# Products with v in groups of five and four key tiles (first batch: two) instead of three (first batch: one)

## The chip, the cores and the metric

The kernel runs on one core of one Trainium2 chip. The metric is the device time of one execution in microseconds (us); lower is better. Three executions of the kernel before gave 1371.67, 1372.15 and 1375.9 us, so the median is 1372.15 us. Engines are named as the profile names them: PE is TensorE (its matmuls), PEld its weight loads, DVE is VectorE, ACT is ScalarE, POOL is GpSimd, SP is SyncE.

## The reference, cut to what matters

All arrays are 32-bit floats. q, k and v have the shape (4, 8, 1152, 64): 4 batches, 8 heads, 1152 positions, 64 features.

```python
q_pool = q.reshape(B, H, S // 2, 2, D).mean(axis=3)           # 576 queries
scores = (1 / sqrt(D)) * q_pool @ k.transpose(0, 1, 3, 2)
attn = exp(scores - max(scores)); attn = attn / (sum(attn) + 1e-09)
x = (attn @ v), heads side by side                            # (2304, 512)
h = x @ moe_w_in;   x = (h - tanh(h)) @ moe_w_out             # 512 -> 2048 -> 512
h = x @ moe2_w_in;  r = max(h, 0)
out = (s * r * r + b) @ moe2_w_out
```

## The kernel before, in words

The 32 heads are taken as 16 pairs; pair n holds heads (n, 0) and (n, 1), and four pairs (NPAIR) make a batch. For each head a loop runs over nine key tiles t of 128 positions (NKT = 9). `scores` (line 380) makes for each half g of the 576 queries the scores transposed, keys on the partitions: two matmuls (lines 386 and 387) into one PSUM tile of 128x288, and ACT takes its exponential into one half of the tile `pf` (line 388). There are three such PSUM tiles and PFB = 10 `pf` tiles.

The scores and both dense layers run in a reduced 32-bit format (one pass over the 288 columns for each matmul). The products of `pf` with v run in full 32-bit format: for one key tile and one half, the 288 columns go through the array in two matmul records.

The products come in two forms:

- In the first batch (n < 4) v has a 65th column of ones, and `single` (line 451) multiplies one key tile: its half 0 into the PSUM tile `pv`, its half 1 into the PSUM tile `su` (line 458), 65 columns of weights each, so that the sum of the exponentials comes out as a 65th row. Between the two halves there is a tick.
- In the later batches `batch` (line 479) multiplies BATCH = 3 key tiles in one go (line 490), 64 columns of weights each: half 0 goes into PSUM partitions 0 to 63, half 1 into 64 to 127, and the two halves run side by side. The sums of the exponentials are made by POOL, which adds the nine `pf` tiles of a head (line 449), and by one product with ones for each head (line 504, `total`), which is put behind the last batch of the head. Only the last head of all (15, 1) has its sums made by PE (line 428).

`batch` is called when more than BATCH tiles are pending, so it runs behind the scores of the tile after its own; `single` when more than LAG = 3 are pending. `batch` puts its matmuls on PE right behind the last matmul of the scores (`issue_after`, with raised priority).

Everything else is woven in by `tick`, four times for each key tile: it runs what was put off (`later`), a step of `prep` for the pair after the next (transposes of q and k, lines 289 and 308; and the maxima of the scores, whose matmuls at line 347 are reduced by DVE at line 348 through three PSUM tiles of the pool psP), and, in the later batches, 111 ns worth of matmuls of the first dense layers (lines 557 and 570), which use psP as well. DVE also turns weights into the reduced format (lines 209 to 221), POOL takes part in this at line 224.

Behind the attention come the two dense stages (line 700 to the end), which the change does not touch.

Of the kernel before, what the change touches and what calls it, by code (L numbers as in the profile page):

```python
# [9 lines left out]
F32 = mybir.dt.float32  # L10
# [8 lines left out]
P = 128  # L19
# [5 lines left out]
LAG = 3  # L25
# [18 lines left out]
SUM = 2  # L44
GROUPS = ((0, 1, 2, 3, 4, 5, 6, 7, 8),)
GROUPS_LAST = ((0, 1, 2, 3, 4), (5, 6, 7, 8))
BATCH = 3
STORE, PUT = 8, 6

MOE_NS = 445  # L50
EVAC_NS = 250
AHEAD = 400
PFB = 10
SOON = 40
HOLD_NS = 8000

# [6 lines left out]
def attention_moe_moe_kernel(  # L63
# [14 lines left out]
    B, H, S, D = q.shape  # L78
# [3 lines left out]
    SQ = S // 2  # L82
    HB = SQ // 2
    NKT = S // P
# [16 lines left out]
    mm = nc.tensor.matmul  # L101
# [21 lines left out]
    for i in range(4):  # L123
        g = i % 2
# [26 lines left out]
    def later(k, fn):  # L151
        queue.append((clock[0] + k, fn))
# [77 lines left out]
    ap = actx.enter_context(tc.tile_pool(name="att", bufs=1, side="right"))  # L230
# [16 lines left out]
    vos = [ap.tile([P, NKT, D + 1], F32, name=f"vo{i}") for i in range(2)]  # L247
# [132 lines left out]
    def scores(n, j, t):  # L380
        T1, U1 = ops[n]
        pf = ap.tile([P, SQ], F32, tag="pf", name=f"pf{n}_{j}_{t}", bufs=PFB)
        for g in range(2):
# [21 lines left out]
    def groups(n, j):  # L405

        return GROUPS_LAST if (n, j) == (len(pairs) - 1, 0) else GROUPS

    def plain(n, j):

        return (n, j) == (len(pairs) - 1, 1)

    fresh = []
    sums = {}

    def sum_plain(n, j, t0):


        if t0 == 0:
            return  # L420
        if (n, j) not in sums:
            sums[n, j] = psV.tile([P, HB], F32, tag="su", name=f"su{n}_{j}")
        su = sums[n, j]
        while fresh and fresh[0][:2] == (n, j) and fresh[0][2] < t0 + BATCH:
            _, _, u, pf = fresh.pop(0)
            for g in range(2):
                o = 32 * (2 * (u % 2) + g)
                mm(su[o:o + 32], ones[:, 0:32], pf[:, g * HB:(g + 1) * HB],
                   start=(u < 2), stop=(u >= NKT - 2))
        if t0 == NKT - BATCH:  # L430
            later(1, lambda: spread_plain(n, j))

    def spread_plain(n, j):
        sx = fp.tile([P, HB], F32, tag="sx", name=f"sx{n}_{j}")
        act(sx, sums.pop((n, j)), AF.Copy)
        pt = psP.tile([P, KB], F32, tag="pp", name=f"pts{n}_{j}")
        mm(pt[:, :HB], spread, sx, start=True, stop=True)
        end(n, j, pt[:, :HB])

    last = [None]  # L440
    pvt, accs, due = {}, {}, []
    placed = []

    def add(n, j, t, r, pf):

        old = accs[n, j, r]
        if t == groups(n, j)[r][1]:
            accs[n, j, r] = ap.tile([P, SQ], F32, tag="acc", name=f"acc{n}_{j}_{r}", bufs=4)
        added[0] = pool.tensor_add(accs[n, j, r], old, pf)  # L449

    def single():

        n, j, t, pf = pend.popleft()
        if t == 0:
            pvt[n, j] = [psV.tile([P, HB], F32, tag=x, name=f"{x}{n}_{j}") for x in ("pv", "su")]
        po = pvt[n, j]
        for g in range(2):
            mm(po[g][0:D + 1], vos[j][:, t], pf[:, g * HB:(g + 1) * HB],  # L458
               start=(t == 0), stop=(t == NKT - 1))
            yield  # L460
        if t == NKT - 1:
            later(0, lambda: finish_single(n, j))

    def finish_single(n, j):
        xv = xvs[n, j] = fp.tile([P, HB], F32, tag="xv", name=f"xv{n}_{j}", bufs=3)
        po = pvt.pop((n, j))
        for g in range(2):
            act(srow[D:D + 1, g], po[g][D:D + 1], AF.Copy)
            act(xv[g * D:(g + 1) * D], po[g][0:D], AF.Copy)

        def total():
            pt = psP.tile([P, KB], F32, tag="pp", name=f"pts{n}_{j}")
            for g in range(2):
                mm(pt[:, :HB], rows[g], srow[:, g], start=(g == 0), stop=(g == 1))
            end(n, j, pt[:, :HB])

        later(2, total)

    def batch():


        todo = [pend.popleft() for _ in range(BATCH)]
        n, j, t, _ = todo[0]
        if t == 0:
            pvt[n, j] = psV.tile([P, HB], F32, tag="pv", name=f"pv{n}_{j}")
        po = pvt[n, j]
        with tc.high_priority(offset=AHEAD), tc.issue_after(last[0].ins):
            for i, (_, _, u, pf) in enumerate(reversed(todo)):
                for g in (1, 0):
                    mm(po[g * D:(g + 1) * D], vos[j][:, u, 0:D], pf[:, g * HB:(g + 1) * HB],  # L490
                       start=(t == 0 and i == 0), stop=(u == NKT - BATCH))
            total()
            if plain(n, j):
                sum_plain(n, j, t)
        if t == NKT - BATCH:
            later(0, lambda: finish_head(n, j))

    def total():
        for n, j in due:
            su = psV.tile([P, HB], F32, tag="su", name=f"su{n}_{j}")  # L500
            nr = len(groups(n, j))
            for r in range(nr):
                for g in (1, 0):
                    mm(su[g * D:(g + 1) * D], ones, accs[n, j, r][:, g * HB:(g + 1) * HB],
                       start=(r == 0), stop=(r == nr - 1))
            later(0, lambda: end(n, j, su))
        due.clear()
# [3 lines left out]
    def finish_head(n, j):  # L511

        xv = xvs[n, j] = fp.tile([P, HB], F32, tag="xv", name=f"xv{n}_{j}", bufs=3)
        act(xv, pvt.pop((n, j)), AF.Copy)
# [81 lines left out]
    pend = deque()  # L596

    def add_prep(n):
        preps.append([prep(n), clock[0]])
# [4 lines left out]
    def fill(ns):  # L604
        credit[0] += ns
        while moe and credit[0] > 0:
            try:
                ns = next(moe[0])
                credit[0] -= ns
                done[0] += ns if ns == 123 else 0  # L610
            except StopIteration:
                moe.popleft()
        credit[0] = min(credit[0], 0)

    def tick():

        clock[0] += 1
        due = [x for x in queue if x[0] <= clock[0]]
        queue[:] = [x for x in queue if x[0] > clock[0]]
        for _, fn in due:  # L620
            fn()
        for p in list(preps):
            if p[1] <= clock[0]:
                try:
                    p[1] = clock[0] + next(p[0])
                except StopIteration:
                    preps.remove(p)
        if done[0] < total_ns - HOLD_NS:
            fill(MOE_NS / 4)
# [13 lines left out]
    for n in range(len(pairs)):  # L643
        b, hp = pairs[n]
        if n == 0:
            add_prep(1)
        for j in range(2):
            for t in range(NKT):
                if j == 1 and t == NKT - LEAD // 4 and n + 2 < len(pairs):
                    add_prep(n + 2)  # L650
                if t == LAG + 1:
                    if j == 1 and n + 1 < len(pairs):
                        preps.append([prep_head(n + 1, 0), clock[0]])
                    if j == 0 and n > 0:
                        preps.append([prep_head(n, 1), clock[0]])
                if hp == 1 and j == 0 and t == 0 and b > 0:
                    while moe:
                        fill(1000)
                    moe.extend(sweep1(b - 1, g) for g in range(2))
                while (n, j) not in ready:  # L660
                    tick()
                for _ in scores(n, j, t):
                    tick()
                if pend[0][0] < NPAIR:
                    if len(pend) > LAG:
                        for _ in single():
                            tick()
                    else:
                        tick()
                        tick()  # L670
                else:
                    tick()
                    if len(pend) > BATCH:
                        batch()
                    tick()
                if (n, j, t) in early1:
                    with tc.issue_after(newest[0].ins) if n == 0 else ExitStack():
                        w1gen.step()
                if n == len(pairs) - 1 and (n, 1) in ready:
                    if FW not in slots:  # L680
                        pctx.close()
                        wpc = ctx.enter_context(tc.tile_pool(name="wc", bufs=1, reuse_waits="tile"))
                        new_slots(wpc, range(FW, FA))
                    w1gen.step()
# [91 lines left out]
    pend = deque()  # L776
# [50 lines left out]
    for i in range(NBLK):  # L827
# [3 lines left out]
        for f in range(NFC):  # L831
            assert w2gen.left <= 2 * (NFC - 1 - f) or not w2gen.left
            ps = hidden(weight(1, f), cur, NB, f"2_{i}_{f}")
            r = mp_.tile([P, NB], F32, tag="th", name=f"r{i}_{f}")
# [46 lines left out]
```

## Time and profile before

| | |
|---|---|
| median of three runs | 1372.15 us |
| the profiled execution | 1372.28 us, its span 1370.5 us |
| instructions in the span | 22374 |
| PE busy | 1336.5 us, 98% of the span |
| DVE, ACT, POOL busy | 63%, 42%, 30% |
| mean granted TensorE clock | 0.996 |
| products with v, first batch (line 458) | 288 matmul records, from 33.1 to 184.3 us |
| products with v, later batches (line 490) | 864 matmul records, from 185.2 to 639.0 us |

Times in the trace are counted from the start of the span. The attention ends at about 641 us. A matmul's shown duration holds its way through the array, which overlaps the next matmul: what a matmul costs in a full stream is the distance from its start to the next start. A timeline row with "x12" merges twelve neighbours: its start is that of the first, and the next row's start tells when the following matmul began.

### The profile page before, as it was taken

The page shows a single profiled execution, that of the slowest core. Times are in us where ns is not written, and L with a number is a line of the kernel's source. Part 1 is how long each engine was busy: PE and PEld are TensorE (multiplying, and loading weights), DVE is VectorE, ACT ScalarE, POOL GpSimd, SP SyncE. Part 2 cuts the span into 40 slices and gives each one's busy share as a digit, 9 for nine tenths or more (in the row PEclk, how much of TensorE's full clock was granted, in tenths as well). Part 3 has the DMA queues.
Part 4 walks back from the last instruction along what each step waited for, and adds up shares of the span by engine and source line. Part 5 has one row for each costly group of instructions (what it writes and reads, how often), then busy time and mean ns, then how long its engine had stood idle before and what let it go on. Part 6 is the DMA issues. An engine that isn't in the chain of part 4 may idle for free.

```text
span 1370.5 us, 22374 instructions
## 1 busy us (share of the span) xinstructions
PE 1336.5 (98%) x8262; PEld 1153.4 (84%) x8262; DVE 870.1 (63%) x1643; ACT 572.7 (42%) x1408; POOL 411.7 (30%) x333
## 2 busy tenths in 40 slices
PE   7999998999999999998999999999999999999998
PEld 4777766777777777776999999999999999989997
DVE  6887779776566665768898668886873232323332
ACT  2455554555555555553333333443332222323222
POOL 0221166667677666773222111110120000000000
PEclk9999999999999999999999999999999999999999
DMA  8677766575656666454785226665421101010000
GB/s 187 150 167 167 168 143 141 133 180 135 165 112 157 139 152 152 100 130 120 249 254 191 97 66 194 203 200 166 158 79 37 47 24 46 24 46 24 1 24 23
DMA packets 190413, 169.58 MB, mean 124 GB/s; under 512 B 88928, under 2 KB 166880, under 8 KB 190304
## 3 DMA queue, kind: packets, MB, share of 16 engines
q1 hardware_dynamic: 187968, 167.56, 46.4%
q8 instruction: 65, 1.06, 0.3%
q10 hardware_dynamic: 2336, 0.59, 0.2%
q14 instruction: 44, 0.36, 0.1%
HBM read 101.98 MB, written 30.67 MB: 97 GB/s over the span
## 4 chain that ended last, share of the span: by engine, by line
PE 86%; DVE 7%; DMA 3%; issue 1%; ACT 1%; POOL 0%; SPq 0%; ACTq 0%; DVEq 0%; POOLq 0%
PE h L744 26%; PE o L817 15%; PE y L755 11%; PE pv L490 7%; PE ptm L347 5%; PE s L386 5%; PE s L387 5%; PE y L570 3%; PE h L557 3%; PE pv L458 2%; PE su L458 2%; DVE ri L523 1%; PE ptk L308 1%; DVE mp L348 1%; DMA raw<-in_moe_w_out_dram 1%
## 5 line engine op out<-in xcount | busy, mean ns | idle before, releaser
L744 PE MATMUL h<-xx,w 128*128 128x288 f32 (+1 forms) x2256 | 373.3, 314 | 0.9 <-DMA xx<-x1d 0.9
L744 PEld LDWEIGHTS h<-xx,w 128*128 128x128 f32 x2256 | 350.6, 188 | 8.9 <-DMA xx<-x1d 1.1
L388 ACT ACTIVATE pf<-s 128x288 f32<-128x288 f32 x576 | 219.1, 410 | 139.0 <-PE s L387 131.5
L348 DVE TENSOR_REDUCE mp<-ptm 128x1 f32<-128x384 f32 x384 | 204.0, 548 | 89.7 <-PE ptm L347 81.4
L449 POOL TENSOR_TENSOR acc<-acc,pf 128x576 f32<-128x576 f32 x159 | 229.6, 1444 | 61.5 <-ACT pf L388 53.8
L224 POOL TENSOR_TENSOR w<-t,w 128x512 fp32r<-128x512 f32 (+1 forms) x80 | 89.1, 1114 | 428.5 <-ACT w L223 278.4
L386 PE MATMUL s<-U,T 128*128 128x288 f32 x576 | 185.9, 330 | 1.5 <-ACT pf L388 0.9
L755 PE MATMUL y<-ghb,w 128*128 128x288 f32 x784 | 171.8, 296 | 0.0
L387 PE MATMUL s<-U,T 65*128 65x288 f32 x576 | 171.5, 307 | 0.1
L817 PE MATMUL o<-w,g2h 128*128 128x512 f32 x540 | 169.3, 395 | 0.0
L347 PE MATMUL ptm<-T,U 128*128 128x384 f32 x360 | 139.4, 393 | 6.3 <-DVE mp L348 3.1
L836 DVE SCALAR_TENSOR_TENSOR r<-r,sb 128x384 f32<-128x384 f32 x96 | 59.2, 618 | 134.2 <-ACT r L835 134.1
L755 PEld LDWEIGHTS y<-ghb,w 128*128 128x128 f32 x784 | 130.4, 188 | 0.2 <-DVE yr L763 0.2
L841 DVE SCALAR_TENSOR_TENSOR g2l<-r,sb,g2h 128x384 fp32r<-128x384 f32 x96 | 61.3, 638 | 105.7 <-ACT g2h L840 105.7
L386 PEld LDWEIGHTS s<-U,T 128*128 128x128 f32 x576 | 111.2, 194 | 18.0 <-ACT pf L388 6.2
L490 PE MATMUL pv<-pf,vo 128*64 128x288 f32 x864 | 121.0, 415 | 0.0
L387 PEld LDWEIGHTS s<-U,T 65*128 65x128 f32 x576 | 110.8, 194 | 7.2 <-issue 4.4
L817 PEld LDWEIGHTS o<-w,g2h 128*128 128x128 f32 x540 | 100.6, 188 | 16.9
L755 PE MATMUL y<-glb,w 128*128 128x288 f32 x392 | 114.6, 292 | 0.0
L835 ACT ACTIVATE r<-h 128x384 f32<-128x384 f32 x96 | 47.1, 491 | 154.1 <-PE h L744 153.7
L817 PE MATMUL o<-w,g2l 128*128 128x512 f32 x270 | 106.9, 396 | 0.0
L840 ACT ACTIVATE g2h<-r,sb 128x384 fp32r<-128x384 f32 x96 | 59.4, 619 | 111.5 <-PE o L817 107.9
(102 smaller groups left out, 1886.1 us busy)
## 6 DMA issues: line engine op xcount, KB each, us to landing
xx<-x1d SPq DMA_DIRECT2D x80, 288.0 KB
T<-T SPq DMA_DIRECT2D x50, 288.0 KB
raw<-in_moe_w_in_dram SPq DMA_DIRECT2D x23, 512.0 KB
raw<-in_moe_w_out_dram SPq DMA_DIRECT2D x23, 512.0 KB
qr<-in_q_dram SPq DMA_DIRECT2D x32, 288.0 KB
vo<-in_v_dram SPq DMA_DIRECT2D x32, 288.0 KB
x1d<-xo SPq DMA_DIRECT2D x64, 144.0 KB
x2d<-xo SPq DMA_DIRECT2D x32, 288.0 KB
```

Of the source, the lines that this page charges most:

```text
L224: added[0] = pool.tensor_sub(w[:, 2 * i + 1, cols], x, f32(w[:, 2 * i, cols]))
L347: mm(pt, U1[j][:, q0:q0 + P], T1[j][:, kk], start=True, stop=True)
L348: newest[0] = dve.reduce_max(mp[:, s, i:i + 1], pt, axis=AX.X)
L386: last[0] = mm(ps, T1[j][:, t * P:(t + 1) * P], U1[j][:, sl], start=True, stop=False)
L387: last[0] = mm(ps, T2[j][:, t * P:(t + 1) * P], U2[j][:, sl], start=False, stop=True)
L388: act(pf[:, sl], ps, AF.Exp, scale=SCALE)
L449: added[0] = pool.tensor_add(accs[n, j, r], old, pf)
L490: mm(po[g * D:(g + 1) * D], vos[j][:, u, 0:D], pf[:, g * HB:(g + 1) * HB], start=(t == 0 and i == 0), stop=(u == NKT - BATCH))
L744: mm(ps[:, :n], w[:, a, c * P:(c + 1) * P], xx[:, c, x, 0:n], start=(i == 0 and c == 0), stop=(i == 2 and c == NDC - 1))
L755: mm(ys[i][c], w[:, a, c * P:(c + 1) * P], x, start=(f == fa and r == 0), stop=(f == fb - 1 and r == 2))
L817: mm(ys[i][r], x[:, r * P:(r + 1) * P], w[:, a], start=(f == 0 and n == 0), stop=(f == NFC - 1 and n == 2))
L841: dve.scalar_tensor_tensor(out=gl, in0=r, scalar=sb2[:, 1:2], in1=f32(gh), op0=ALU.add, op1=ALU.subtract)
```

## The change

The products with v are taken in other groups. In the later batches a head's nine tiles are taken as five and four (SPLIT), except the last head (15, 1), which keeps three times three (SPLIT_LAST). In the first batch `single` takes two tiles at once (PAIRED; the ninth tile is alone), later one before the other, without a tick between the halves, and right behind the last scores; it is called when more than four tiles are pending instead of three. One more `pf` tile (PFB = 11) is paid for with one fewer accumulator of POOL (`acc`, three instead of four). The accumulation flags follow the groups.

```diff
-BATCH = 3
+SPLIT = (5, 4)
+SPLIT_LAST = (3, 3, 3)
+PAIRED = 2
...
-PFB = 10
+PFB = 11
...
-            accs[n, j, r] = ap.tile([P, SQ], F32, tag="acc", name=f"acc{n}_{j}_{r}", bufs=4)
+            accs[n, j, r] = ap.tile([P, SQ], F32, tag="acc", name=f"acc{n}_{j}_{r}", bufs=3)
...
     def single():
-        n, j, t, pf = pend.popleft()
+        n, j, t, _ = pend[0]
+        todo = [pend.popleft() for _ in range(min(PAIRED, NKT - t))]
         if t == 0:
             pvt[n, j] = [psV.tile([P, HB], F32, tag=x, name=f"{x}{n}_{j}") for x in ("pv", "su")]
         po = pvt[n, j]
-        for g in range(2):
-            mm(po[g][0:D + 1], vos[j][:, t], pf[:, g * HB:(g + 1) * HB],
-               start=(t == 0), stop=(t == NKT - 1))
-            yield
-        if t == NKT - 1:
+        with tc.issue_after(last[0].ins):
+            for _, _, u, pf in reversed(todo):
+                for g in range(2):
+                    mm(po[g][0:D + 1], vos[j][:, u], pf[:, g * HB:(g + 1) * HB],
+                       start=(t == 0 and u == todo[-1][2]), stop=(u == t and todo[-1][2] == NKT - 1))
+        if todo[-1][2] == NKT - 1:
             later(0, lambda: finish_single(n, j))
...
+    def size(n, j, t):
+        split = SPLIT_LAST if plain(n, j) else SPLIT
+        return split[[sum(split[:i]) for i in range(len(split))].index(t)]
+
     def batch():
-        todo = [pend.popleft() for _ in range(BATCH)]
-        n, j, t, _ = todo[0]
+        n, j, t, _ = pend[0]
+        todo = [pend.popleft() for _ in range(size(n, j, t))]
+        end_ = todo[-1][2] == NKT - 1
...
-                       start=(t == 0 and i == 0), stop=(u == NKT - BATCH))
+                       start=(t == 0 and i == 0), stop=(end_ and i == len(todo) - 1))
             total()
             if plain(n, j):
-                sum_plain(n, j, t)
-        if t == NKT - BATCH:
+                sum_plain(n, j, t, todo[-1][2] + 1)
+        if end_:
             later(0, lambda: finish_head(n, j))
...
                 if pend[0][0] < NPAIR:
-                    if len(pend) > LAG:
-                        for _ in single():
-                            tick()
-                    else:
-                        tick()
-                        tick()
+                    tick()
+                    if len(pend) > LAG + PAIRED - 1:
+                        single()
+                    tick()
                 else:
                     tick()
-                    if len(pend) > BATCH:
+                    if len(pend) > size(*pend[0][:3]):
                         batch()
                     tick()
```

## Rows read from the trace of the kernel before

**Rows 1.** Windows: length, busy us (x instructions) per engine, granted clock, DMA share, GB/s.

```profile
33.00:185.00 152.00, 150.09 (x792) 114.38 (x791) 122.67 (x281) 83.85 (x225) 31.05 (x37) 1.00 0.74 166
185.00:262.00 77.00, 68.35 (x431) 51.36 (x431) 62.30 (x108) 38.73 (x107) 54.00 (x42) 0.96 0.56 127
262.00:600.00 338.00, 334.71 (x2275) 263.30 (x2272) 224.55 (x405) 185.03 (x511) 237.07 (x178) 1.00 0.62 143
```

**Rows 2.** Line 490 by itself: its instructions, and its weight loads in two of those windows.

```profile
L490 PE MATMUL pv<-pf,vo x864: 406/406/744, 185.2 to 639.0; 128*64 128x288 f32 x173
...
185.00:262.00 77.00, 19.95 (x142) 9.39 (x144) 0.96 0.56 127
262.00:600.00 338.00, 89.28 (x640) 40.90 (x636) 1.00 0.62 143
```

**Rows 3.** PE timeline (start, us, line, tiles, count), a batch of three tiles alone.

```profile
610.99 0.29 PE L387 MATMUL s<-U,T 65*128 65x288 f32 x1
611.21 1.68 PE L490 MATMUL pv<-pf,vo 128*64 128x288 f32 x12
612.82 0.67 PE L557 MATMUL h<-xx,w 128*128 128x288 f32 x3
613.32 0.29 PE L386 MATMUL s<-U,T 128*128 128x288 f32 x1
```

**Rows 4.** PE timeline, a batch with the product with ones behind it.

```profile
600.50 0.30 PE L387 MATMUL s<-U,T 65*128 65x288 f32 x1
600.72 1.68 PE L490 MATMUL pv<-pf,vo 128*64 128x288 f32 x12
602.23 0.66 PE L504 MATMUL su<-acc,ones 128*64 128x288 f32 x4
602.82 0.44 PE L347 MATMUL ptm<-T,U 128*128 128x384 f32 x1
603.09 0.29 PE L570 MATMUL y<-gla,w 128*128 128x288 f32 x1
```

**Rows 5.** PE timeline of the first batch, one tile's products between scores.

```profile
151.07 0.65 PE L458 MATMUL pv<-pf,vo 128*65 128x288 f32 x2
151.56 0.65 PE L458 MATMUL su<-pf,vo 128*65 128x288 f32 x2
...
152.31 0.30 PE L386 MATMUL s<-U,T 128*128 128x288 f32 x1
152.44 0.30 PE L387 MATMUL s<-U,T 65*128 65x288 f32 x1
152.58 0.65 PE L458 MATMUL pv<-pf,vo 128*65 128x288 f32 x2
```

**Rows 6.** The same with two matmuls of line 347 in the round.

```profile
155.49 0.34 PE L347 MATMUL ptm<-T,U 128*128 128x384 f32 x1
155.67 0.29 PE L386 MATMUL s<-U,T 128*128 128x288 f32 x1
...
155.93 0.65 PE L458 MATMUL pv<-pf,vo 128*65 128x288 f32 x2
...
157.78 0.65 PE L458 MATMUL pv<-pf,vo 128*65 128x288 f32 x2
```

**Rows 7.** The two longest waits of PE in 185 to 262 us: total us, times, longest us.

```profile
PE ptm L347 <- DVE tha L584: 2.9, 1, 2.9
PE ptk L308 <- DVE mp L348: 2.4, 1, 2.4
```

**Rows 8.** Waits of PE in 262 to 600 us.

```profile
PE y L570 <- DVE gla L588: 1.0, 3, 0.4
PE ptm L347 <- DVE mp L348: 0.8, 3, 0.3
PE y L570 <- DVE mp L348: 0.4, 2, 0.2
```

**Rows 9.** Waits of PE in 600 to 645 us.

```profile
PE su L504 <- POOL acc L449: 2.9, 1, 2.9
```

More of the change, by code (lines that the diff above doesn't have):

```diff
@@ L414, in attention_moe_moe_kernel, with sum_plain @@
     sums = {}
-    def sum_plain(n, j, t0):
+    def sum_plain(n, j, t0, t1):
         if t0 == 0:
@@ L423, in sum_plain @@
         su = sums[n, j]
-        while fresh and fresh[0][:2] == (n, j) and fresh[0][2] < t0 + BATCH:
+        while fresh and fresh[0][:2] == (n, j) and fresh[0][2] < t1:
             _, _, u, pf = fresh.pop(0)
@@ L429, in sum_plain @@
                    start=(u < 2), stop=(u >= NKT - 2))
-        if t0 == NKT - BATCH:
+        if t1 == NKT:
             later(1, lambda: spread_plain(n, j))
```

## The prediction

> **What bounds the kernel now.** I read the windows first, then the timeline of PE around the products, then the waits. The windows [rows 1] show where PE has no time to spare: in the first batch it is busy for 150.09 of 152 us, in the long middle of the attention for 334.71 of 338 us, while DVE, ACT and POOL each have at least a fifth of the time free. Between 185 and 262 us it is different: PE lacks 8.65 us, and DVE is busy for 62.30 of 77 us. So in the middle a microsecond taken from PE's own stream shortens the run, and in the short stretch it may only lengthen a wait.
>
> Then the price of a matmul as the distance from start to start. A reduced-format matmul of 288 columns costs (152.58 - 152.31) / 2 = 0.135 us, and one full-format record (151.56 - 151.07) / 2 = 0.245 us [rows 5]. A matmul of line 347 costs 155.67 - 155.49 = 0.18 us [rows 6].
>
> **What a group of three costs beyond its matmuls.** From 610.99 to 613.32 us are 2.33 us [rows 3]. In them start four reduced-format matmuls (one of line 387, three of line 557: 0.54 us) and a batch of 12 records. Its halves run side by side, so these are 6 x 0.243 = 1.46 us. 2.33 - 0.54 - 1.46 = 0.33 us are left. They lie at both ends: the batch starts 0.22 us after line 387 instead of 0.135, and the rest comes after it. The batch with the product with ones [rows 4] gives the same: 603.09 - 600.50 = 2.59 us, less 0.135, less 8 x 0.243 = 1.94, less 0.18 for line 347, is 0.33 us. So a batch pays 0.33 us once, whether it has 6 or 8 steps. No engine is named in these rows as late, so this is paid by PE itself on the way into the side-by-side form and out of it.
>
> **Later batches: 23 groups fewer.** Line 490 has 864 records at 12 a batch [rows 2]: 72 batches, three for each of 24 heads. 23 heads go to two, the last keeps three: 49 batches. 23 x 0.33 = 7.6 us less on PE; the number of matmuls stays. All of it lies on the path where PE is the bound. By window: 144 / 12 = 12 batches, four heads, lie in 185 to 262 us; 636 / 12 = 53 in 262 to 600 us [rows 2].
>
> What can eat of this: in 185 to 262 us PE waits 2.9 us once for the gate's subtraction and 2.4 us once for a reduction of the maxima [rows 7], both on DVE. If DVE's chain sets those moments, the four groups saved there (1.3 us) lengthen the waits. The same holds for the one group saved in head (15, 0): PE waits 2.9 us for POOL's last sum [rows 9]. So between 0 and 1.7 us of the 7.6 is lost; without a row that tells which, I take the middle, 0.9 us.
>
> What a longer batch adds: five tiles keep PE away from scores, maxima and dense work for 5 x 2 x 0.243 + 0.33 = 2.8 us instead of 1.8. ACT and DVE run dry for that time, and afterwards PE may wait for them. Today this costs almost nothing: in 262 to 600 us all waits of PE for DVE are 1.0 + 0.8 + 0.4 = 2.2 us [rows 8], 0.04 us for each of the 53 batches. Batches get longer by half and fewer by a third, so I cost this at zero. The bounds are a gain of those 2.2 us and a loss of the same size. The cover is the free third of DVE (224.55 of 338 us) and the 45% of ACT [rows 1]. The call comes, as before, one tile after the group's last scores, so it waits for no younger exponential; and the last group of a head is still called behind the first scores of the next head, so POOL's sums are due at the same tile.
>
> The buffers are costed at nothing. Up to six tiles are pending instead of four, and PFB grows by one, which leaves five `pf` tiles for ACT to run ahead instead of six; ACT runs about one tile ahead. An accumulator lives from a head's second tile to the first tile of the next head, so at most two are alive. If either were short, ACT or POOL would stop for one batch, 2.8 us at most, and PE after them.
>
> **First batch: no switch to save, some evenness to lose.** Here 72 groups become 8 x (4 + 1) = 40, but rows 5 show no price of a group. One round from 151.07 to 152.58 us lasts 1.51 us and holds four reduced-format matmuls (0.54 us) and four records (0.98 us): 1.52 us. With line 347 between the halves [rows 6] there are even two groups in a round: 157.78 - 155.93 = 1.85 us against 0.54 + 0.98 + 0.36 = 1.88 us. With 65 columns the halves do not run side by side, and entering and leaving is free. So nothing is removed on PE.
>
> The Trainium skill agrees on this point: its page TensorEngine Tiling (Key Properties) says that a change of the tiling mode, not of the tile alone, drains TensorE, and under When to Use Tiling it gives 64 columns or fewer as the case for column tiling. By that rule 65 columns change no mode and the 32 groups saved here are worth nothing; by the opposite reading, in which any change of form costs what a batch costs, they would be worth 10.6 us. The rounds above side with the first.
>
> What is added is a wait in line: eight records, 8 x 0.245 = 1.96 us, in one piece instead of two pieces of 0.49 us with a step of line 347 between them. Queued behind them on PE are the next maxima, for which DVE waits, and the next scores, for which ACT waits. DVE is the one to watch: 122.67 of 152 us busy here [rows 1], 81%. The bounds: PE can gain no more than the 1.9 us that it lacks in this window; and at the other end, if DVE had nothing to spare, the additional 4 x 0.245 = 0.98 us of every pair would be lost, 32 x 0.98 = 31 us. The nearest row is the middle of the attention, where pieces of 1.5 to 2 us already interrupt the same loop at 0.04 us each: 32 x 0.04 = 1.3 us. I take that, since it is the same loop with the same three PSUM tiles, and DVE is only somewhat fuller.
>
> **Sum.** -7.6 + 0.9 + 0 + 1.3 = -5.4 us. The profiled execution took 1372.28 us (0.13 us above the median of the three runs), so 1366.9 us. Both dense stages behind the attention keep their length and only start earlier.
>
> **The rivals.**
>
> *The gain is absorbed.* PE gets ahead, and what empties its PSUM tiles does not. For it: the 5.3 us and 2.9 us of waits for DVE and POOL that exist already [rows 7, 9], and that a burst empties DVE's queue. Against it: 2.2 us of such waits in the 338 us that hold 53 of the 72 batches [rows 8]. Here the rest would be 0 to 4 us of gain, in the middle 1370.3 us. The Trainium skill speaks for this rival: TensorEngine Tiling (PSUM Bottleneck) warns that a faster TensorE leaves the emptying of PSUM as it was, and that the copies can become the bound; the windows show that they are not in the middle stretch. To this rival also belongs that the longer groups do not stay whole on PE.
>
> *The first batch gets slower by more than the later ones gain.* One mechanism: in the piece of 1.96 us DVE runs out of maxima, its conversions are queued behind the reductions that it waits for, and the lost time comes back as waits of PE for psP. The later batches bring 7.6 - 0.9 = 6.7 us, so it decides from 6.7 / 32 = 0.21 us per pair; at 0.45 us, half of what a pair can lose, it is 32 x 0.45 = 14.4 us, and the time 1372.28 - 6.7 + 14.4 = 1380.0 us. For it: DVE's 81%. Against it: 29 us of DVE's window are free.
>
> *Every group costs, in the first batch too.* Then 32 x 0.33 = 10.6 us more go: 1372.28 - 6.7 - 10.6 = 1355.0 us. Against it stand the two rounds that add up without it [rows 5, 6].
>
> **How the numbers follow.** Forecast 58%, absorbed 25%, slower 11%, larger gain 6%. About 0.3% is what a measurement of this kernel can tell from no change: 4.1 us, so faster is below 1368.0 us and slower above 1376.3 us. The forecast's own range is 1363 (the full 7.6 us and the 1.9 us of the first batch) to 1369 (1.7 us absorbed and 2.5 us lost in the bursts). Of its 58 some 8 lie above 1368.0; faster is then 50 + 6 + 5 from the upper part of the absorbed cases = 61%. Slower is 9 of the 11; the other 30% are no change. For 8 in 10 the range must take in nearly all of the absorbed case: 1361 to 1373 us. Its low end also lets the wait of rows 9 go.
>
> **What would show it.** Right: line 490 keeps 864 records in 49 batches; a batch of five takes 0.33 us beyond 10 x 0.243 us; PE's busy time falls by about what the time falls; the stretch from 262 to 600 us is shorter by some 5.5 to 6 us, and the stretch from 33 to 185 us longer by 1 to 2 us, with new waits of line 347 for line 348. Wrong: if the first batch gets shorter by more than 2 us, groups there did cost something; if waits of PE for DVE or ACT in the middle grow beyond 4 us, the bursts matter; if a batch of five costs much more than 0.33 us beyond its matmuls, the price is not one for each group.

## The result, and the profile after

The changed kernel took 1383.3 us in the median of five runs (1382.43 to 1389.7) against 1372.15 us: a ratio of 1.0087 [1.0059, 1.0115]. It is slower by 11 us where 5.4 us of gain were forecast, and it lies above the range of 1361 to 1373 us. The profiled execution is the longest of the five, 1389.7 us, with a span of 1387.9 us at a granted clock of 0.989; before had 0.996. A second profile of the same kernel (label x1, below) has a span of 1381.5 us at 0.993.

The windows of [rows 1], now of the changed kernel. The columns are window and length, busy time and instructions of PE, PEld, DVE, ACT and POOL, granted clock, DMA share, GB/s:

```profile
33.00:185.00 152.00, 151.24 (x779) 110.54 (x778) 123.01 (x281) 79.35 (x220) 29.72 (x35) 1.00 0.71 164
185.00:262.00 77.00, 67.88 (x397) 49.98 (x395) 61.35 (x104) 35.76 (x102) 51.26 (x41) 0.89 0.53 120
262.00:600.00 338.00, 325.07 (x2214) 260.56 (x2214) 224.16 (x392) 179.58 (x501) 230.62 (x174) 0.99 0.61 139
```

In the first batch PE is as full as before. In the middle, 262 to 600 us, it is busy for 325.07 us instead of 334.71: work went out of it, and holes came in. What PE waits for in that window, where [rows 8] show it for the kernel before (total us, times, longest us):

```profile
PE ptk L310 <- DVE mp L350: 3.6, 1, 3.6
PE ptc L354 <- DVE m L352: 3.4, 2, 1.7
PE ptm L349 <- DVE mp L350: 3.4, 6, 0.9
```

The waits for DVE are 10.4 us instead of 2.2 (the 3.6 us lie in the end of pair 5). The worst window is 185 to 262 us, where the clock fell from 0.96 to 0.89. A window with fixed ends does not say how long a piece of work takes, so the table cuts the traces at the first score matmul of a head (us; (1, 0) is pair 1's first head; "alone" are two experiments below):

| stage | before | change | change, x1 | pairs alone, e1 | five/four alone, e2 |
|---|---|---|---|---|---|
| start to (1, 0) | 68.0 | 71.8 | 70.8 | 71.5 | 67.6 |
| pairs 1 to 3 | 110.2 | 109.9 | 109.9 | 110.1 | 110.1 |
| pair 4 | 34.7 | 27.8 | 27.8 | 33.9 | 31.2 |
| pair 5 | 47.0 | 62.6 | 58.8 | 46.9 | 42.6 |
| pairs 6 to 14 | 340.1 | 343.1 | 343.2 | 341.7 | 348.0 |
| pair 15 and the rest | 770.5 | 772.7 | 771.2 | 770.7 | 769.9 |

Three places lose: some 3 us in pair 0, 5 to 9 us in pairs 4 and 5 together, and 3 us in pairs 6 to 14, where 18 groups fewer should have brought 6. Each column is one trace. That of e2 is the fastest of eleven executions (1371.15 to 1379.53 us, median 1374.53), so its stretches show less loss than its median has. In pairs 6 to 14 the traces with groups of three and POOL's additions lie between 340.1 and 342.2 us.

The gain itself is there. The products of the later batches, by line (count, shortest, median and longest duration in ns, first and last start in us, form):

```profile
L500 PE MATMUL pv<-pf,vo x864: 406/406/742, 190.2 to 654.1; 128*64 128x288 f32 x173
```

The same 864 records, now in 49 batches (23 of 20 records, 23 of 16, three of 12). One batch of five in PE's timeline (start, duration, engine, line, operands):

```profile
335.21 0.30 PE L389 MATMUL s<-U,T 65*128 65x288 f32 x1
335.44 2.65 PE L500 MATMUL pv<-pf,vo 128*64 128x288 f32 x20
338.01 0.44 PE L349 MATMUL ptm<-T,U 128*128 128x384 f32 x1
338.29 0.29 PE L388 MATMUL s<-U,T 128*128 128x288 f32 x1
338.42 0.29 PE L389 MATMUL s<-U,T 65*128 65x288 f32 x1
```

From 335.21 to 338.42 are 3.21 us. Less two score matmuls (0.27), one maximum (0.18) and ten steps of 0.243, 0.33 us are left, as in [rows 3, 4].

### The profile page after: what moved, and what is told of

It reads as the page before. It is cut to its first block, busy times and chain, and to the rows that moved or that the text cites. A ratio compares the mean times of both kernels' runs of the same rounds, so it can differ in the third digit from the quotient of the medians.

```text
span 1387.9 us, 22327 instructions
## 1 busy us (share of the span) xinstructions
PE 1344.8 (97%) x8262; PEld 1159.1 (84%) x8262; DVE 878.7 (63%) x1643; ACT 567.0 (41%) x1408; POOL 412.2 (30%) x333
## 4 chain that ended last, share of the span: by engine, by line
PE 86%; DVE 7%; DMA 3%; ACT 2%; issue 1%; POOL 1%; SPq 0%; ACTq 0%; DVEq 0%; POOLq 0%
PE h L752 26%; PE o L825 14%; PE y L763 11%; PE pv L500 6%; PE s L388 5%; PE ptm L349 5%; PE s L389 4%; PE y L580 3%; PE pv L463 3%; PE su L463 2%; PE h L567 2%; DVE mp L350 2%; PE ptk L310 1%; ACT pf L390 1%; DVE gla L598 1%
## 5 line engine op out<-in xcount | busy, mean ns | idle before, releaser
L390 ACT ACTIVATE pf<-s 128x288 f32<-128x288 f32 x576 | 214.1, 410 | 115.6 <-PE s L389 110.1
L388 PE MATMUL s<-U,T 128*128 128x288 f32 x576 | 182.9, 327 | 3.0 <-ACT pf L390 2.7
L500 PE MATMUL pv<-pf,vo 128*64 128x288 f32 x864 | 118.2, 419 | 0.0
```

Of the source, the lines that this page charges most:

```text
L388: last[0] = mm(ps, T1[j][:, t * P:(t + 1) * P], U1[j][:, sl], start=True, stop=False)
L390: act(pf[:, sl], ps, AF.Exp, scale=SCALE)
```

## The experiments

Each diff is against the changed kernel, unless it says otherwise. Ratios are to the kernel before, run on the same chip.

**x1: the change again.** No edit.

> The changed kernel once more, as the measure for the parts. Measured so far 1383.3 us against 1372.15 us, so about +11 us. The trace of the changed kernel puts +4 us into the first batch (head (0, 0): scores of pair 1 come 4 us later), about +7 to +15 us into the four heads of pairs 4 and 5 (where DVE is busy for 28.46 of 30.9 us and the granted clock falls to 0.73), and about +3 us into the 320 us behind, where 18 groups fewer should have brought -6 us. Theory A (the loss is made where DVE is late): the slow stretch shows again in heads (5, 0) and (5, 1). Theory B (chance of the clock): this time the stretch is as long as before and the time is below 1376 us.

1384.97 us, 1.0093 [1.0078, 1.0108]. The loss repeats; pair 5 is 58.8 us instead of 62.6, so some of the first profile's length is scatter.

**e3, e2, e1: the parts alone.** e3 is the kernel before with PFB = 11 and three accumulators. e2 has the change's SPLIT and buffers, and `single` as before. e1 has the pairs, with groups of three and the old buffers:

```diff
-SPLIT = (5, 4)
+SPLIT = (3, 3, 3)
-PFB = 11
+PFB = 10
...
-            accs[n, j, r] = ap.tile([P, SQ], F32, tag="acc", name=f"acc{n}_{j}_{r}", bufs=3)
+            accs[n, j, r] = ap.tile([P, SQ], F32, tag="acc", name=f"acc{n}_{j}_{r}", bufs=4)
```

> The kernel before with 11 pf tiles and 3 accumulators and nothing else; its PE order is the same as before. The prediction and theory A: no change, within 1.5 us. A rival in which the accumulator that is missing makes POOL wait: slower by 2 us or more.

> Only the later batches are changed (five and four, 11 pf tiles, 3 accumulators); the first batch keeps one tile at a time. The prediction: -7 us. Theory A: the groups bring -7.9 us on PE, but the waits for DVE in pairs 4 and 5 and in the middle give back all of it and more: 0 to +8 us. If the time is 5 us or more below that of the kernel before, the loss belongs to the first batch alone.

> Only the first batch is changed (two key tiles at once); the later batches keep three times three, 10 pf tiles and 4 accumulators. Theory A, with its part in the first batch: +3 to +5 us, nearly all between 35 and 72 us. The prediction: +1.3 us. The rival that every group costs: -10 us. If the later stretch at pairs 4 and 5 also grows here, it comes from the order in which the first batch leaves the work of the preparation, not from the longer batches.

e3 1373.23 us, 1.0003 [0.9994, 1.0011]; e2 1374.53 us, 1.0018 [1.0006, 1.003]; e1 1377.36 us, 1.0032 [1.002, 1.0045]. The buffers cost nothing. The two parts alone lose 2.5 and 4.4 us; the whole loses 12.8 in x1, more than their sum: pair 5 grows in neither part alone.

**e4, e9, e15: what the pairs cost.** The table puts e1's loss before (1, 0), not into pairs 1 to 3. e4 is e1 with pair 0 taken one tile at a time; e9 is e1, and e15 the change, without the order that puts the products right behind the newest scores:

```diff
# e4
-        todo = [pend.popleft() for _ in range(min(PAIRED, NKT - t))]
+        todo = [pend.popleft() for _ in range(min(PAIRED if n else 1, NKT - t))]
...
-                    if len(pend) > LAG + PAIRED - 1:
+                    if len(pend) > LAG + (PAIRED if pend[0][0] else 1) - 1:
# e9, e15
-        with tc.issue_after(last[0].ins):
+        with ExitStack():
```

> The pairs of key tiles in the first batch begin with pair 1; pair 0 keeps one tile at a time; later batches as before. With pairs everywhere it was +4.4 us, of which the trace has +3.6 us between the first scores of head (0, 0) and those of head (1, 0). Theory: the loss is made once, at the start, because fewer products are ready to fill PE while it waits for the first data of pair 1: now within 1.5 us of the kernel before. Rival (each pair of tiles costs something): still +3 us or more.

> Pairs of key tiles in the first batch as in e1, but without the edge that puts them behind the last scores; later batches as before. In e1 the products of the last tiles of head (0, 0) stand on PE behind the scores of pair 1, which wait for their data. Theory: that edge is the whole loss of the first batch, so the first scores of head (1, 0) come at most 1 us later than in the kernel before (e1: 3.6 us later) and the time is within 2 us of it. Rival (the pairs delay, since they are taken a tile later): as e1, +4 us.

> The whole change without the edge that puts the pairs of the first batch behind the last scores. If the edge is the cause of what the two halves cost beyond their sum, the time falls to 1374 to 1378 us and pair 5 to below 48 us. If not, 1381 us or more, with pair 5 near 58 us.

e4 1375.14 us, 1.0015 [1.0003, 1.0027]; e9 1374.14 us, 1.0014 [1.0004, 1.0023]; e15 1382.13 us, 1.0074 [1.0055, 1.0094]. From the first scores of (0, 1) to those of (1, 0) it takes 16.8 us in before, 19.9 to 21.1 in the kernels with the order (e1, change, x1, and e4 with single tiles), 17.4 and 17.5 without it (e15, e9). So within head (0, 1) it is the order that costs 3 us, not the length of the pair: e4's theory, a loss made by pairs in pair 0, is wrong. Without the order a part of it only moves ahead, to head (0, 0): the first scores of (1, 0) come at 70.6 us in e9 and 69.0 in e15, against 71.5 in e1, 71.8 and 70.8 in the change, and 67.6 to 69.2 in before and six kernels with its first batch (e2, e3, e7, e8b, e11, e14). e9 expected them at most 1 us later than before, and they are 2.6 us later. At the end of head (0, 0), PE before:

```profile
48.50 0.55 PE L347 MATMUL ptm<-T,U 128*128 128x384 f32 x1
48.89 0.65 PE L458 MATMUL pv<-pf,vo 128*65 128x288 f32 x2
49.16 0.55 PE L347 MATMUL ptm<-T,U 128*128 128x384 f32 x1
49.55 0.65 PE L458 MATMUL su<-pf,vo 128*65 128x288 f32 x2
```

and PE of the changed kernel:

```profile
48.20 0.65 PE L463 MATMUL su<-pf,vo 128*65 128x288 f32 x2
48.47 0.90 PE L349 MATMUL ptm<-T,U 128*128 128x384 f32 x3
49.68 2.31 PE L349 MATMUL ptm<-T,U 128*128 128x384 f32 x5 [0.30 <-DVE mp L350]
51.82 0.56 PE L388 MATMUL s<-U,T 128*128 128x288 f32 x3
...
53.56 0.65 PE L463 MATMUL pv<-pf,vo 128*65 128x288 f32 x2
```

Before, a product fills PE while DVE reduces each maximum. After, the head's last products are held behind scores of the next head, which start at 51.82 us. Until then PE has only maxima left, those of pair 1; it runs eight of them in a row at DVE's pace and does the products later. e15 is still slow: pair 5 is 60.6 us without the order.

**e5, e6, e6b, e16: the conversions of weights.** CONVERT says how many conversions of dense weights (lines 211 to 223 of DVE; lines 209 to 221 in the kernel before) are called in each pair. In the changed kernel's heads (4, 1), (5, 0) and (5, 1) (columns as above):

```profile
195.60:209.50 13.90, 13.03 (x87) 9.16 (x85) 9.79 (x16) 7.39 (x21) 13.18 (x11) 1.00 0.65 156
209.50:240.40 30.90, 24.02 (x141) 18.17 (x141) 28.46 (x51) 12.52 (x35) 19.28 (x17) 0.89 0.64 142
240.40:272.10 31.70, 27.01 (x138) 21.67 (x137) 23.91 (x38) 12.01 (x34) 14.44 (x11) 0.73 0.33 82
```

In (5, 0) DVE is busy for 28.46 of 30.9 us; some 16 us of it are 21 operations of conversions, against 8 us and 13 in before. Pair 4 is 7 us shorter than in before, and this work is still there behind it. DVE around 210 us, then what PE waits for from 185 to 275 us (total, times, longest):

```profile
210.56 1.43 DVE L218 TENSOR_SCALAR raw<-raw 128x256 int32<-128x256 int32 x1
211.91 0.28 DVE L211 TENSOR_SCALAR t<-raw 128x256 int32<-128x256 int32 x1
212.11 1.62 DVE L220 SCALAR_TENSOR_TENSOR t<-raw,t 128x256 f32<-128x256 int32 x1
213.65 0.54 DVE L350 TENSOR_REDUCE mp<-ptm 128x1 f32<-128x384 f32 x1
```

```profile
PE ptk L310 <- DVE mp L350: 3.6, 1, 3.6
PE ptm L349 <- DVE mp L350: 2.7, 4, 1.9
PE ptq L291 <- DVE mp L350: 2.4, 1, 2.4
PE ptm L349 <- DVE mp L324: 2.1, 1, 2.1
```

The 2.4 us end when the reduction that had to wait for the conversion is done (214.2 us). Around such waits the granted clock is at its lower level, 1.2 GHz:

```profile
213.90:220.70 6.80, 6.44 (x25) 4.46 (x27) 5.51 (x13) 2.62 (x7) 1.93 (x2) 0.50 0.43 125
241.20:251.40 10.20, 9.38 (x32) 7.32 (x32) 7.76 (x15) 1.27 (x4) 2.60 (x3) 0.50 0.21 55
265.10:271.90 6.80, 6.01 (x25) 6.00 (x26) 3.80 (x8) 2.41 (x6) 1.41 (x1) 0.50 0.33 84
```

These are 23.8 us; x1 has 13.7 us of it in the two pairs and before 6.8. So the conversions were moved into the first batch, in before (e5, e16), in the change (e6) and in e2 (e6b):

```diff
-CONVERT = (4, 4, 4, 4, 2, 2, 0, 0, 0, 1, 1, 1, 1)
+CONVERT = (5, 5, 5, 5, 0, 0, 0, 0, 0, 1, 1, 1, 1)
# e16
+CONVERT = (6, 6, 6, 6, 0, 0, 0, 0, 0, 0, 0, 0, 0)
```

> The kernel before, with the weight conversions of pairs 4 and 5 (two each) moved to pairs 0 to 3 (five each instead of four). It is the measure for the next two. Theory: DVE has 29 us free in the first batch, so the four conversions cost nothing there, and pairs 4 and 5 get shorter by 2 to 6 us: 1367 to 1371 us.

> The changed kernel with the same move of the conversions. Theory (pair 5 is slow because DVE has conversions to do there while the maxima wait, and the clock falls in the waits): pair 5, 58.8 us in the last trace of the changed kernel, falls to 46 us or less, and the whole to 1372 to 1377 us. Rival (the longer batches themselves hold up the maxima): pair 5 stays above 52 us and the time above 1380 us.

> Five and four in the later batches alone, one tile at a time in the first, with the same move of the conversions. Theory: 1362 to 1368 us if pairs 4 and 5 are where the gain is lost; if the loss in pairs 6 to 14 (11 us of new waits in the trace of five and four alone) is a thing of its own, 1366 to 1372 us, no better than the kernel before with the same move by more than 2 us.

> The kernel before (groups of three) with all 24 early weight conversions in pairs 0 to 3 (six each), none from pair 4 on. Theory: DVE's work beside POOL's additions is what PE waits for in pairs 4 and 5, so these get no longer than with five each, pairs 9 to 12 lose their one step each, and the first batch, where DVE still has time, grows by at most 3 us: 1363 to 1368 us, against 1367.1 us with five each. Rival (the first batch is full): 1369 us or more.

e5 1367.07 us, 0.9956 [0.994, 0.9973]; e6 1377.35 us, 1.003 [1.002, 1.004]; e6b 1377.26 us, 1.0027 [1.0014, 1.0039]; e16 1366.38 us, 0.9959 [0.9945, 0.9973]. Pair 5 falls from 58.8 (x1) to 50.0 us in the change and from 47.0 to 42.6 in before: the conversions there cost time in both. But they are a small part of the loss. Against e5, which has the same move, e6 is still slower by 10.3 us, where x1 is slower than before by 12.8; and its pair 5 lies between the 46 us of the theory and the 52 of the rival. e6b is a miss, and slower than e5 by 10.2 us: its pair 5 is longer than e2's (46.6 against 42.6 us), and nothing is gained. e16 is 0.4% faster than before, as e5 is; its pairs 4 and 5 in three windows (from 194 us, in pair 4, to the first scores of pair 6):

```profile
194.00:212.80 18.80, 18.21 (x120) 12.90 (x117) 12.57 (x23) 10.82 (x32) 17.73 (x15) 1.00 0.48 111
212.80:234.70 21.90, 21.43 (x140) 16.80 (x140) 15.34 (x30) 10.78 (x30) 16.70 (x13) 1.00 0.81 176
234.70:252.10 17.40, 17.37 (x120) 13.16 (x120) 11.04 (x23) 11.18 (x32) 11.26 (x9) 1.00 0.38 101
```

PE is busy throughout and the clock stays at 2.4 GHz. This was found beside the change and owes it nothing.

**e7, e8b, e12, e13: relieving DVE in the middle.** In its trace e2 gains 8.4 us up to the first scores of (6, 0) and has lost it again by the end of pair 14; some 2 us of that are work of PE that it does behind the first scores of (6, 0) instead of ahead of them (nine matmuls of the first dense layer, six transposes, three maxima). What weight loads wait for from 177 to 600 us, in before and then in e2 (total, times, longest):

```profile
PEld ptm L347 <- DVE mp L348: 6.3, 12, 2.0
...
PEld s L386 <- ACT pf L388: 4.9, 15, 0.8
```

```profile
PEld ptm L349 <- DVE mp L350: 13.5, 23, 3.6
PEld ptc L354 <- DVE m L352: 5.9, 4, 2.0
...
PEld s L388 <- ACT pf L390: 4.3, 16, 0.5
PEld s L389 <- DMA U<-c: 4.1, 5, 1.9
```

One case, PE and then DVE of e2:

```profile
416.33 2.65 PE L498 MATMUL pv<-pf,vo 128*64 128x288 f32 x20
418.90 0.62 PE L349 MATMUL ptm<-T,U 128*128 128x384 f32 x2
...
422.53 0.27 PE L354 MATMUL ptc<-ident,m 128*4 128x128 f32 x1 [1.69 <-DVE m L352]
```

```profile
418.05 1.70 DVE L536 TENSOR_TENSOR xv<-xv,ri 128x288 f32<-128x288 f32 x1
419.67 1.68 DVE L596 TENSOR_TENSOR gla<-tha,gha 128x288 fp32r<-128x288 f32 x1
421.27 1.01 DVE L350 TENSOR_REDUCE mp<-ptm 128x1 f32<-128x384 f32 x2
422.31 0.17 DVE L352 TENSOR_REDUCE m<-mp 128x4 f32<-128x12 f32 x1
```

The last two maxima of the block stand behind the 2.65 us of products; when they are made, two operations of 1.7 us stand ahead of their reductions on DVE, and the transpose of the maxima waits 1.69 us. In before the same two operations come behind the maxima (DVE, then PE), and the transpose does not wait:

```profile
422.28 0.15 DVE L350 TENSOR_REDUCE m<-mp 128x4 f32<-128x12 f32 x1
422.36 1.67 DVE L528 TENSOR_TENSOR xv<-xv,ri 128x288 f32<-128x288 f32 x1
```

```profile
423.58 0.27 PE L352 MATMUL ptc<-ident,m 128*4 128x128 f32 x1
```

Such operations are long while POOL adds `pf` tiles. So seven of POOL's eight additions for each head were left out (the sums are then of two tiles only), in before (e7) and e2 (e8b); e12 and e13 are these two with a maximum taken over 96 of 384 columns as well:

```diff
# e7, e8b
-        else:
+        elif t == gr[r][1]:
             later(SUM, lambda: add(n, j, t, r, pf))
# e12, e13 also
-                    newest[0] = dve.reduce_max(mp[:, s, i:i + 1], pt, axis=AX.X)
+                    newest[0] = dve.reduce_max(mp[:, s, i:i + 1], pt[:, 0:96], axis=AX.X)
```

> The kernel before without most of POOL's sums: of the eight additions of a head (line 449) one is left, so the divisor is not the whole sum. It is the measure for the next run. In the traces DVE operations on two tiles take 1.7 us instead of 0.45 us while POOL adds; without the additions PE should wait less in pairs 4 to 14: 1355 to 1368 us.

> The same omission with groups of five and four in the later batches. Theory (a saved group is worth 0.345 us, and what takes it back are reductions on DVE that stand behind operations stretched by POOL's additions): without the additions the gain appears, 5 to 8 us less than the run without additions and with groups of three. Rival (it is the length of the burst itself, or the order on PE, that costs): within 3 us of it.

> The kernel before with one of POOL's eight additions of a head left (the divisor is not the whole sum) and with the maxima taken over 96 of 384 columns (an exponent's offset that is not the true maximum). The measure for the next run; both engines that PE waits for have far less to do: 1340 to 1353 us.

> The same omissions with groups of five and four. Theory (what eats the gain are waits of PE for the reductions on DVE): now the gain shows, 5 to 8 us less than the run before it. Rival (the longer stretches without a batch between the scores flood ACT's three PSUM tiles and leave PE without filler, whatever DVE does): within 3 us of it.

e7 1352.68 us, 0.9857 [0.9842, 0.9872]; e8b 1352.86 us, 0.9859 [0.9844, 0.9873]; e12 1355.15 us, 0.9869 [0.9849, 0.989]; e13 1349.12 us, 0.9829 [0.9811, 0.9847]. e7 is below its 1355 to 1368 us. Without the additions five/four no longer loses to groups of three, but it does not gain the 5 to 8 us of e8b's theory either. With short maxima as well it wins, by 6 us in the medians (four executions each, 1346.1 to 1352.4 us against 1350.7 to 1357.8). For groups of three the short maxima bring nothing: e12 missed its 1340 to 1353 us, and its first scores of (1, 0) come at 73.5 us, in e7 at 67.6. PE's waits for DVE in pairs 6 to 14 are 2.2 us in before, 8.1 in e2, 6.9 in x1, 0.6 in e8b and 0.2 in e13.

**e11, e14: other pieces.** `single` as before.

```diff
# e11, with PFB = 10 and four accumulators
-SPLIT = (5, 4)
+SPLIT = (2, 2, 2, 2, 1)
# e14
+SPLIT = (5, 2, 2)
```

> Later batches in groups of 2, 2, 2, 2 and 1 key tiles, so 46 groups more than before (the last head keeps three times three); the rest as before. If PE's own price of a group is all, +46 x 0.345 = +15.9 us. If shorter pieces let DVE and ACT go on more evenly, so that waits fall as they rose with longer ones (about +10 us of waits for 23 groups fewer), the time rises by 5 us or less.

> Later batches in groups of 5, 2 and 2 key tiles: as many groups as before, the same price on PE, but the longest piece is five tiles as in the change. If the length of a piece is what costs (waits of about 10 us for five and four, 9 us fewer for twos), it is slower than the kernel before by 3 to 6 us. If the waits come only from having PE ahead by the saved groups, it is within 1.5 us of it.

e11 1379.39 us, 1.0055 [1.0039, 1.0072]; e14 1377.78 us, 1.0036 [1.0023, 1.0048]. e14 has as many groups as before and pays no more for entries, but loses 5 us, as expected if a long piece costs by itself. e11 is between its two theories. The table takes the stretch from the first scores of (4, 0) to those of (15, 0), against the kernel with groups of three and otherwise the same edits (421.8 us in before, 415.2 in e5, 405.5 in e7, 401.7 in e12), with 65 groups there and 0.345 us for each (the median distance lost in the batches of these traces). "Left" is the rest of the sum; it is not a wait by itself. What of it shows as idle time of PE stands beside it.

| kernel | groups | stretch | price of groups | left | idle PE |
|---|---|---|---|---|---|
| twos, e11 | 109 | +7.8 | +15.2 | -7.4 | -2.5 |
| five, two, two, e14 | 65 | +4.7 | 0 | +4.7 | +2.4 |
| five and four, e2 | 43 | -0.1 | -7.6 | +7.5 | +5.0 |
| five and four, conversions moved, e6b | 43 | +8.6 | -7.6 | +16.2 | +10.0 |
| five and four, no additions, e8b | 43 | -3.0 | -7.6 | +4.6 | +1.1 |
| and short maxima, e13 | 43 | -3.9 | -7.6 | +3.7 | +0.5 |
| the whole change, x1 | 43 | +7.8 | -7.6 | +15.4 | +9.1 |
| the whole change, conversions moved, e6 | 43 | +4.1 | -7.6 | +11.7 | +7.3 |

Pairs 6 to 14 are the steadier part of it. There the whole change loses 3.0 us, twice, instead of gaining 6.2, and e2 and e6b lose 7.9 and 5.7; without the additions (e8b) it is 0.5 lost, each of these three with some 2 us of moved work; with short maxima as well (e13) it is 3.6 gained. e14 loses 1.9 us there, no more than kernels with groups of three differ, and twos 11.9, nearly their price of 12.4: what e14 loses and twos win back lies mostly in pairs 4 and 5.

## Why the prediction was wrong

- *The price of a group* (0.33 us, 23 groups, 7.6 us): right, by the batch at 335 us and by the 864 records. The price is the same, 0.34 to 0.35 us in the median, in batches of two, three, four and five tiles (e11, before, change).
- *No price of a group with 65 columns:* right. 24 groups fewer in pairs 1 to 3 change 110.2 us to 109.9. The rival by which every group costs falls with it.
- *"What a longer batch adds", costed at zero with 2.2 us as bounds:* this is the step that failed. In pairs 6 to 14 of the change, where no clock falls and PE has the same matmuls to do, it measured 9.2 us (3.0 lost where 6.2 were to be gained), 6.2 of them as idle PE. The small waits of [rows 8] were scaled by the number of batches, as if a batch were only an interruption. But it is also what PE does while ACT and DVE catch up; behind a longer one the maxima come to DVE late, and stand behind operations that POOL's additions stretch. Shown: in the middle five/four loses less without these additions and wins with short maxima as well, and PE's waits for DVE go from 8.1 to 0.6 and 0.2 us (e2, e8b, e13). Not shown: why of the 6.2 us only 3.6 are won in e13, though PE is hardly idle there (the longer runs of scores between the batches, for which ACT has three PSUM tiles, are a guess); and why five, two, two costs so much less there than five and four. The cover named, DVE's free third, is an average: in (5, 0) DVE is 92% busy. (In the first batch it has 19% free, a little less than the fifth that was read there.)
- *Absorbed, 0.9 us in pairs 4 and 5:* the change loses 4.8 to 8.7 us there, in conversions, late maxima and a clock at its lower level. But the parts alone gain there, e2 8.0 us (2 of them moved work) and e1 0.8: with the conversions where they were, the loss comes only with both. [Rows 7] were read as a cap on the gain, when they are a load that a faster pair 4 runs into.
- *The first batch, 1.3 us for 32 pairs:* mis-sized and misplaced. Pairs 1 to 3 cost nothing; e1's 4.4 us lie mostly in head (0, 1), where the order behind the last scores costs 3 us. Without the order e9 still loses 1.9 us of the 4.4, so the order is a part of the cause. The prediction took `single` as moved by one tile and asked only what waits behind it, not what it waits behind.
- *Buffers at nothing:* right (e3).
- *The rivals:* "absorbed" comes nearest to e2, whose loss of 2.5 us lies beyond its 0 to 4 us of gain. "Slower" had the sign, but its mechanism, DVE starved by every pair of the first batch, did not occur: pairs 1 to 3 are as long as before.
- *What would show it:* the sign named for wrong, waits of PE for DVE in the middle that grow beyond 4 us, is what came (from 2.2 to 10.4 us in 262 to 600 us; 6.9 of it in pairs 6 to 14).

Open: why pairs in the first batch and longer batches together make pair 4 run ahead so far (27.8 us, against 33.9 and 31.2 alone; it is not the order of the products: e15), and why e6b gains nothing. So the whole change's 15 us beyond the price of groups are located, 9 of them in pairs 6 to 14 and 6 in pairs 4 and 5, with conversions as a part of the cause in pairs 4 and 5 (e6), but not fully explained.

## What to carry to other kernels

Work that fills PE between the pieces that feed other engines can be worth more spread out than in one block: before merging it to save a fixed price, ask who is fed in the gaps and what else that engine has queued at that moment, and try one run with the same number of pieces in uneven lengths. A free third of an engine over a long window covers nothing if the work comes in bursts; look at the window of one head. When a product is tied behind the newest instruction, look also at when that instruction can run, and at what is left to fill PE until then.

## What the runs showed of the hardware

Operations of DVE with two tiles in SBUF become longer while POOL adds; line 596 takes on average twice its time. In e2 and then, without seven of eight additions, in e8b, from 185 to 600 us (count, busy us and mean ns, idle before):

```profile
L596 DVE TENSOR_TENSOR gla<-tha,gha 128x288 fp32r<-128x288 f32 x25 | 26.5, 1059 | 5.3 <-ACT gha L595 5.2
```

```profile
L596 DVE TENSOR_TENSOR gla<-tha,gha 128x288 fp32r<-128x288 f32 x26 | 13.6, 523 | 5.9 <-ACT gha L595 5.2
L218 DVE TENSOR_SCALAR raw<-raw 128x256 int32<-128x256 int32 x7 | 2.0, 286 | 0.0
```

The reductions of the maxima, which read PSUM (line 350), do not: 548 and 549 ns on average. Line 218, 286 ns on average in e8b, took 1.43 us in the changed kernel at 210.56 us, beside these additions of POOL:

```profile
210.24 4.75 POOL L451 TENSOR_TENSOR acc<-acc,pf 128x576 f32<-128x576 f32 x3
```

The first of the three ends at 211.84 us and the second at 213.45; line 218 ends at 211.99 us and line 220 at 213.73, each just behind one of them. Line 211, which starts at 211.91 us, 0.01 us before the second, takes its usual 0.28 us.

Leaving the additions out shortens the kernel by 20 us (e7), though POOL is busy for 30% of the span and PE seldom waits for it. The Trainium skill (SBUF — State Buffer, section "SBUF: two separate sides") says that a GpSimd operation that reads SBUF and an operation of VectorE with two inputs in SBUF lock each other out of a shared port pair for a whole instruction, and that one in a two-port mode does so too. Lines 596 and 220, with their two inputs, agree. Line 218 reads one tile, and no row names its mode; undisturbed it takes 0.29 us for its 256 columns (46.57 us in the changed kernel) where line 220, with two tiles, takes 0.42 (45.36 us).
